# Linear attention and a maxout layer on one core: transposes from TensorE to crossbar DMAs, stores over all DMA engines, state sums by 64-row tiles

## The chip, the cores and the metric

One core of a Trainium2 chip runs the whole program. The metric is the device time of one execution in microseconds (us). A core has TensorE (PE, matmuls; PEld is its weight load), VectorE (DVE), ScalarE (ACT), GpSimd (POOL), SyncE (SP, here the queue that issues most of the DMAs), and 16 DMA engines. Each engine runs its own instructions strictly in order and waits at semaphores for the others.

## The reference, cut to what matters

```
B, H, S, D = 4, 8, 768, 48
state = zeros(B, H, D, D)
for t in range(S):
    cur = einsum('bhd,bhe->bhde', u * k[t], v[t])
    y[t] = einsum('bhd,bhde->bhe', r[t], state + cur)
    state = w[t][..., None] * state + einsum('bhd,bhe->bhde', k[t], v[t])
x = y as (B*S, H*D) = (3072, 384)
out = maximum(x @ w1, x @ w2) @ w_out          # d_ff = 1024
```

The recurrence is computed by chunks of C = 256 time steps. Inside a chunk, r' = r * exp(sum of log w so far) and k' = k * exp(-that sum) turn the decay into plain products. The maxout is computed as relu(x (w1 - w2)) w_out + x (w2 w_out).

## The kernel before, in words

There are 12 units of work, n = 0 to 11: chunk c = n // 4 of batch row b = n % 4, all 8 heads, 256 time steps. Two neighbouring steps lie in one partition (the index i), and a unit has two 64-partition halves (the index b of the code, Q = 64). A name such as `kp.5` is the operation `kp` on unit 5. The order in which all operations are issued is written out by hand in the string ORDER; every engine takes its own instructions in that order and never out of it. PSUM and SBUF tiles come from pools with fixed numbers of buffers.

The steps of a unit, with the engine of each:

- `w k r v`: loads of 384 KB each, issued by SP, three buffers each. `lw` (ACT) log w, `lp` (POOL) pair sums, `cs` (PE) running sums, `AE`, `AO`, `iA` (ACT) exponentials, `m`, `z` (DVE) sums.
- `rp`, `kp` (DVE, L262 and L266): r' and k' in bf16, both into `rkn_b`, two buffers. `rk`, `rku`, `vb`, `vd` (POOL) and `dg` (DVE): the part of the present step.
- `tr`, `evr` and `tk`, `evk`: r' and k' transposed by TensorE through an identity matrix, eight 128x128 transposes each (L317), into the single PSUM tile `tr`, and copied out by DVE (L330, L339) as `rT` and `kT`.
- `kv` (PE, L352): k'v into the PSUM tile `y`: j = 0 is the sum over the first 64 partitions, j = 1 the sum over all 128. `S1` (DVE, L362) is the state in the middle of the chunk, `Tf` (L369) at its end. `row`, `WL` (SP) and `Wt` (ACT) move one row of decays onto partitions through DRAM, `dec`, `S0` (POOL) decay the state.
- `sc0`, `sc1` (PE, L393): scores from `kT` and `rT`; `M0`, `M1` (DVE, L397): the mask. `yb`, `yi`, `ya` (PE, L413, L425, L437): the attention output, which `x` (ACT, L446) copies to SBUF.
- `xt`, `xT`: the attention output transposed by TensorE (L453, six 128x128 transposes) and copied out of PSUM by ACT (L458).
- `g0` to `g3` (PE, L466) and `r0` to `r3` (ACT, L474): 24 gate matmuls and the relus. `oc`, `oa`, `ob` (PE, L485, L490), `os` (ACT, L495) and `out` (SP, L500): two output blocks of 128 rows a unit, each stored as 192 KB.

Before the units run evenly, the weights come in: `w1` (SP), `w2` and `wo` (POOL DMAs that cast to bf16), `wd` (DVE, w1 - w2), `wt` (SP crossbar DMA, w2 transposed, three of 128x1024), `wcm` and `wce` (w2 w_out). Units overlap: while the attention of unit n + 2 is built, the gates and outputs of unit n run.

Of the kernel before, what the change touches and what calls it, by code (L numbers as in the profile page):

```python
# [17 lines left out]
w.0 k.0 lw.0 lp.0 cs.0 r.0 u v.0 w2 rk.0 rku.0 vb.0 AE.0 z.0 m.0 AO.0 rp.0 tr.0 iA.0 kp.0 evr.0  # L18
kv.0 Tf.0 tk.0 evk.0 dg.0 sc1.0 M1.0 S1.0 row.0 sc0.0 M0.0 vd.0 yb.0 yi.0 w1 w.1 lw.1 k.1 r.1
v.1 lp.1 wd.1 wd.0 wo w.2 cs.1 AE.1 m.1 AO.1 rp.1 z.1 row.1 wd.2 rk.1 rku.1 ya.0 x.0 tr.1 vb.1  # L20
wt.1 iA.1 k.2 r.2 v.2 w.3 wt.0 wt.2 xt.0 xT.0 g0.0 g1.0 r0.0 g2.0 r2.0 WL.1 WL.0 k.3 r.3 v.3 w.4
dg.1 vd.1 evr.1 kp.1 tk.1 evk.1 kv.1 Tf.1 S1.1 sc1.1 M1.1 yb.1 yi.1 k.4 r.4 v.4 lw.2 lp.2 w.5
cs.2 m.2 AE.2 z.2 row.2 AO.2 rp.2 iA.2 kp.2 sc0.1 M0.1 rk.2 rku.2 k.5 r.5 tr.2 evr.2 r1.0 g3.0
r3.0 wcm.1 wce.1 WL.2 lw.3 lp.3 ya.1 x.1 tk.2 evk.2 vb.2 dg.2 vd.2 v.5 w.6 wcm.0 wce.0 Wt.0 cs.3
m.3 AE.3 z.3 row.3 wcm.2 wce.2 sc0.2 M0.2 AO.3 rp.3 iA.3 kp.3 Wt.1 dec.1 S0.1 xt.1 xT.1 kv.2
Tf.2 S1.2 oc0.0 oa0.0 ob0.0 oc1.0 os0.0 out0.0 oa1.0 ob1.0 os1.0 out1.0 rk.3 rku.3 k.6 r.6 tr.3
evr.3 WL.3 sc1.2 M1.2 lw.4 lp.4 g0.1 g1.1 tk.3 evk.3 vb.3 r0.1 g2.1 r2.1 dg.3 vd.3 v.6 w.7 r1.1
yb.2 yi.2 ya.2 x.2 cs.4 m.4 AE.4 z.4 row.4 sc0.3 M0.3 AO.4 rp.4 g3.1 r3.1 oc0.1 oa0.1 iA.4 kp.4
xt.2 xT.2 kv.3 Tf.3 S1.3 ob0.1 oc1.1 os0.1 oa1.1 ob1.1 g0.2 out0.1 dec.0 S0.0 rk.4 rku.4 k.7 r.7
tr.4 evr.4 WL.4 sc1.3 M1.3 lw.5 lp.5 os1.1 g1.2 out1.1 r0.2 g2.2 r1.2 tk.4 evk.4 vb.4 r2.2 dg.4  # L30
vd.4 v.7 w.8 yb.3 yi.3 ya.3 x.3 cs.5 m.5 AE.5 z.5 row.5 sc0.4 M0.4 AO.5 rp.5 g3.2 r3.2 oc0.2
oa0.2 iA.5 kp.5 xt.3 xT.3 kv.4 Tf.4 S1.4 ob0.2 oc1.2 os0.2 out0.2 oa1.2 ob1.2 g0.3 rk.5 rku.5
k.8 r.8 tr.5 evr.5 WL.5 sc1.4 M1.4 lw.6 lp.6 Wt.2 dec.2 S0.2 os1.2 g1.3 out1.2 r0.3 g2.3 r1.3
tk.5 evk.5 vb.5 r2.3 dg.5 vd.5 v.8 w.9 yb.4 yi.4 ya.4 x.4 cs.6 m.6 AE.6 z.6 row.6 sc0.5 M0.5
AO.6 rp.6 g3.3 r3.3 oc0.3 oa0.3 iA.6 kp.6 xt.4 xT.4 kv.5 Tf.5 S1.5 ob0.3 oc1.3 os0.3 out0.3
oa1.3 ob1.3 g0.4 rk.6 rku.6 k.9 r.9 tr.6 evr.6 WL.6 sc1.5 M1.5 lw.7 lp.7 Wt.3 dec.3 S0.3 os1.3
g1.4 out1.3 r0.4 g2.4 r1.4 tk.6 evk.6 vb.6 r2.4 dg.6 vd.6 v.9 w.10 yb.5 yi.5 ya.5 x.5 cs.7 m.7
AE.7 z.7 row.7 sc0.6 M0.6 AO.7 rp.7 g3.4 r3.4 oc0.4 oa0.4 iA.7 kp.7 xt.5 xT.5 kv.6 Tf.6 S1.6
ob0.4 oc1.4 os0.4 out0.4 oa1.4 ob1.4 g0.5 rk.7 rku.7 k.10 r.10 tr.7 evr.7 WL.7 sc1.6 M1.6 lw.8
lp.8 Wt.4 dec.4 S0.4 os1.4 g1.5 out1.4 r0.5 g2.5 r1.5 tk.7 evk.7 vb.7 r2.5 dg.7 vd.7 v.10 w.11  # L40
yb.6 yi.6 ya.6 x.6 cs.8 m.8 AE.8 z.8 sc0.7 M0.7 AO.8 rp.8 g3.5 r3.5 oc0.5 oa0.5 iA.8 kp.8 xt.6
# [12 lines left out]
oc1.9 os0.9 out0.9 oa1.9 ob1.9 g0.10 kv.11 S1.11 os1.9 g1.10 out1.9 r0.10 g2.10 r1.10 r2.10
yb.11 yi.11 ya.11 x.11 g3.10 r3.10 oc0.10 oa0.10 xt.11 xT.11 ob0.10 oc1.10 os0.10 out0.10 oa1.10
ob1.10 os1.10 out1.10 g0.11 g1.11 r0.11 g2.11 r1.11 r2.11 g3.11 r3.11 oc0.11 oa0.11 ob0.11
oc1.11 os0.11 out0.11 oa1.11 ob1.11 os1.11 out1.11
# [22 lines left out]
def _body(tc, r, k, v, w, u_in, moe_w1, moe_w2, moe_w_out, out):  # L80
# [179 lines left out]
    @op  # L260
    def rp(n):
        nc.vector.tensor_mul(rkn_b[n % 2][:, 0, :, :, 0:D], byi(U[n]["r"]), U[n]["A"])  # L262

    @op
    def kp(n):
        nc.vector.tensor_mul(rkn_b[n % 2][:, 1, :, :, 0:D], byi(U[n]["k"]), U[n]["iA"])  # L266
# [46 lines left out]
    def transp(n, x):  # L313
        tp = pt_([P, NP, 2, 2, Q], BF16, "tr")
        for i in range(2):
            for p in range(NP):
                nc.tensor.transpose(  # L317
                    tp[:, p, :, i, :],
                    rkn_b[n % 2][:, x, i, 2 * p:2 * p + 2, :].rearrange("s r d -> s (r d)"),
                    ident)  # L320
        return tp

    @op
    def tr(n):
        U[n]["tr"] = transp(n, 0)

    @op
    def evr(n):
# [1 line left out]
        nc.vector.tensor_copy(t, U[n]["tr"])  # L330
# [4 lines left out]

    @op
    def evk(n):
        U[n]["kT"] = t = wt_([P, NP, 2, 2, Q], BF16, "kT")
        nc.vector.tensor_copy(t, U[n]["tk"])  # L339
# [3 lines left out]
    def kv(n):  # L343

        U[n]["kv"] = kp = pt_([P, 2, 512], F32, "y")
        for j in range(1 if last(n) else 2):
            q = slice(0, Q if j == 0 else P)
            for i in range(2):
                for p in range(NP):
                    for e in range(2):  # L350
# [1 line left out]
                        nc.tensor.matmul(  # L352
# [194 lines left out]
```

## Time and profile before

| | |
|---|---|
| time, three runs | 189.21, 189.55, 190.67 us (median 189.55) |
| the profiled execution | 190.6 us, of which the span of the profile is 188.8 us |
| PE busy | 148.2 us, 78% of the span |
| DVE, POOL, ACT busy | 124.8 us, 106.4 us, 88.3 us |
| mean granted TensorE clock | 0.965 |

The profiled execution is 1.8 us longer than the span; that part lies outside what the trace shows. It is 1.05 us above the median of the three runs. Busy matmul time is modelled and overlaps weight loads; what ends a stretch is read from the chain of work that ended last.

### The profile page before, as it was taken

The page shows a single profiled execution, that of the slowest core. Times are in us where ns is not written, and L with a number is a line of the kernel's source. Part 1 is how long each engine was busy: PE and PEld are TensorE (multiplying, and loading weights), DVE is VectorE, ACT ScalarE, POOL GpSimd, SP SyncE. Part 2 cuts the span into 40 slices and gives each one's busy share as a digit, 9 for nine tenths or more (in the row PEclk, how much of TensorE's full clock was granted, in tenths as well). Part 3 has the DMA queues.
Part 4 walks back from the last instruction along what each step waited for, and adds up shares of the span by engine and source line. Part 5 has one row for each costly group of instructions (what it writes and reads, how often), then busy time and mean ns, then how long its engine had stood idle before and what let it go on. Part 6 is the DMA issues. An engine that isn't in the chain of part 4 may idle for free.

```text
span 188.8 us, 4945 instructions
## 1 busy us (share of the span) xinstructions
PE 148.2 (78%) x2080; PEld 102.7 (54%) x2080; DVE 124.8 (66%) x173; ACT 88.3 (47%) x153; POOL 106.4 (56%) x96
## 2 busy tenths in 40 slices
PE   0345347849999999999999999999958599999400
PEld 0133116616567676776767668676746376767200
DVE  7478759466787798988979799798774776200000
ACT  3120134333436766748575574857642355456200
POOL 3853594272489994969878686983039970300000
PEclk9999999996999999999999999999999999999955
DMA  6999998999995568164574476457411111111110
GB/s 161 240 235 366 238 170 137 320 125 309 320 257 152 169 145 234 35 179 121 124 191 126 115 191 162 107 158 198 122 48 50 54 50 54 50 54 47 50 50 32
DMA packets 62454, 28.07 MB, mean 149 GB/s; under 512 B 57432, under 2 KB 61656, under 8 KB 62432
## 3 DMA queue, kind: packets, MB, share of 16 engines
q1 hardware_dynamic: 60992, 26.19, 51.3%
q0 software_dynamic: 1440, 1.57, 5.7%
q8 instruction: 16, 0.26, 0.6%
q14 instruction: 6, 0.05, 0.1%
HBM read 23.81 MB, written 4.73 MB: 151 GB/s over the span
## 4 chain that ended last, share of the span: by engine, by line
PE 54%; issue 6%; POOL 5%; DMA 4%; DVE 2%; ACT 2%; SPq 1%; DVEq 0%; POOLq 0%; ACTq 0%
PE go L466 14%; PE go L490 14%; PE go L485 5%; PE tr L317 4%; DMA lw<-in_w_dram 4%; PE y L352 3%; PE ex L235 3%; PE sc L393 3%; PE y L437 2%; PE y L413 2%; PE go L214 2%; PE y L425 2%; PE ex L453 2%; POOL rku L293 1%; POOL rku L298 1%
## 5 line engine op out<-in xcount | busy, mean ns | idle before, releaser
L466 PE MATMUL go<-xT,wd_sb 128*128 128x256 bf16 x288 | 40.1, 285 | 0.9 <-ACT xT L458 0.9
L474 ACT ACTIVATE gT<-go 128x512 bf16<-128x512 f32 x48 | 28.5, 595 | 18.3 <-PE go L466 17.7
L490 PE MATMUL go<-wo_sb,gT 128*128 128x384 bf16 x192 | 36.8, 326 | 0.0
L466 PEld LDWEIGHTS <-wd_sb 128*128 128x128 bf16 x288 | 27.6, 102 | 7.9 <-issue 1.1
L397 DVE TENSOR_TENSOR M<-sc,mask 128x1024 bf16<-128x1024 f32 x24 | 29.3, 1220 | 3.2 <-PE sc L393 2.7
L309 POOL TENSOR_TENSOR vd<-lv,dg 128x768 bf16<-128x768 f32 x12 | 17.7, 1474 | 23.9 <-DVE dg L304 21.0
L230 POOL TENSOR_TENSOR lp<-lw 128x384 f32<-128x384 f32 x12 | 16.9, 1411 | 17.9 <-ACT lw L225 17.9
L298 POOL TENSOR_TENSOR rku<-rku,u_b 128x768 f32<-128x768 f32 x12 | 24.1, 2010 | 0.9
L317 PE MATMUL tr<-ident,rkn 128*128 128x128 bf16 x192 | 16.7, 237 | 9.8 <-DVE rkn L262 9.6
L490 PEld LDWEIGHTS <-gT 128*128 128x128 bf16 x192 | 18.0, 98 | 11.4
L293 POOL TENSOR_TENSOR rku<-lr,lk 128x768 f32<-128x768 f32 x12 | 22.5, 1876 | 0.2
L262 DVE TENSOR_TENSOR rkn<-lr,A 128x768 bf16<-128x768 f32 x12 | 20.0, 1664 | 2.1 <-ACT A L253 2.1
L317 PEld LDWEIGHTS <-rkn 128*128 128x128 bf16 x192 | 14.0, 107 | 12.3 <-DVE rkn L262 11.0
L495 ACT COPY osb<-go 128x384 f32<-128x384 f32 x24 | 11.5, 479 | 19.2 <-PE go L490 16.6
L266 DVE TENSOR_TENSOR rkn<-lk,iA 128x768 bf16<-128x768 f32 x12 | 19.3, 1604 | 1.3 <-ACT iA L258 1.3
L235 PE MATMUL ex<-lp,triS 128*128 128x384 f32 x24 | 12.2, 595 | 9.4 <-POOL lp L230 9.4
L288 POOL CAST vb<-lv 128x768 bf16<-128x768 f32 x12 | 11.3, 943 | 9.9 <-DMA lv<-in_v_dram 9.5
L225 ACT ACTIVATE lw<-lw 128x768 f32<-128x768 f32 x12 | 10.1, 844 | 13.2 <-DMA lw<-in_w_dram 13.2
L485 PE MATMUL go<-wc_sb,xT 128*128 128x384 bf16 x72 | 15.6, 326 | 0.0
L446 ACT CAST x<-y 128x768 bf16<-128x768 f32 x12 | 9.6, 796 | 11.6 <-PE y L437 11.4
L241 ACT ACTIVATE A<-ex 128x384 f32<-128x384 f32 x12 | 5.9, 490 | 18.1 <-DVE mz L245 11.6
L304 DVE TENSOR_REDUCE dg<-rku 128x16 f32<-128x768 f32 x12 | 11.3, 944 | 3.1 <-POOL rku L298 3.1
(51 smaller groups left out, 188.6 us busy)
## 6 DMA issues: line engine op xcount, KB each, us to landing
lw<-in_w_dram SPq DMA_DIRECT2D x12, 384.0 KB
lk<-in_k_dram SPq DMA_DIRECT2D x12, 384.0 KB
lr<-in_r_dram SPq DMA_DIRECT2D x12, 384.0 KB
...
w_sb<-in_moe_w_dram POOLq DMA_DIRECT2D x1, 768.0 KB, 10.0
wo_sb<-in_moe_w_out_dram POOLq DMA_DIRECT2D x1, 768.0 KB, 7.4
```

The costliest lines, as they stand in the source:

```text
L235: nc.tensor.matmul(t.rearrange("p h d -> p (h d)"), triS, U[n]["lp"].rearrange("p h d -> p (h d)"))
L262: nc.vector.tensor_mul(rkn_b[n % 2][:, 0, :, :, 0:D], byi(U[n]["r"]), U[n]["A"])
L266: nc.vector.tensor_mul(rkn_b[n % 2][:, 1, :, :, 0:D], byi(U[n]["k"]), U[n]["iA"])
L293: nc.gpsimd.tensor_mul(t, U[n]["r"], U[n]["k"])
L298: nc.gpsimd.tensor_mul(t, t, u_b.rearrange("p (h d) -> p h d", h=H).unsqueeze(1).to_broadcast([P, 2, H, D]))
L309: nc.gpsimd.tensor_mul(t.rearrange("p i h d -> p h i d"), U[n]["v"], U[n]["dg"].to_broadcast([P, H, 2, D]))
L317: nc.tensor.transpose(tp[:, p, :, i, :], rkn_b[n % 2][:, x, i, 2 * p:2 * p + 2, :].rearrange("s r d -> s (r d)"), ident)
L397: nc.vector.tensor_mul(t.rearrange("s e p t -> s (e p) t"), U[n]["sc", i].rearrange("s e p t -> s (e p) t"), mask[:, i].rearrange("s i q - ...
L466: nc.tensor.matmul(g[:, f, :], wd_sb[:, ko, fo * P:(fo + 1) * P], U[n]["xT"][:, ko].rearrange("p j t -> p (j t)"), start=(f == 0 and ko == ...
L474: nc.scalar.activation(U[n]["gT"][:, 2 * j:2 * j + 2].rearrange("p f j t -> p f (j t)"), U[n]["g", j], AF.Relu)
L485: nc.tensor.matmul(t, U[n]["xT"][:, ko, b, :], wc_sb[:, ko, :], start=(ko == 0), stop=False)
L490: nc.tensor.matmul(U[n]["o", b], U[n]["gT"][:, fo, b, :], wo_sb[:, fo, :], start=False, stop=(fo == FO - 1))
```

## The change

What it does:

- k' is no longer transposed by TensorE: `evk` is one crossbar DMA on SP's queue from the SBUF tile `k_b` (128x1024 bf16) to `kT`. The matmuls `tk` and the DVE copy are gone.
- The attention output is transposed by one crossbar DMA on SP's queue too: `xT` reads `x` (128x768 bf16). The matmuls `xt` and the ACT copy are gone; the tile's axes are in another order, and so are the slices that the gates and `oc` read.
- r' is still transposed by TensorE; its copy out of PSUM, `evr`, moves from DVE to ACT.
- Each 128-row output block is stored by two DMAs of 64 rows whose outermost axis is the 64 rows; it was one DMA with an outermost axis of 2.
- `kv` sums each 64-partition half by itself (b = 0, 1), the halves in turns. `Sa` (DVE) adds the first half to the state, `S1` is now two copies of `Sa` to bf16, and `Tf` adds the second half to `Sa`.
- `WL` and `Wt` get three buffers, r' and k' tiles of their own, and the whole ORDER is new.

```diff
-    rkn_b = [const.tile([P, 2, 2, H, DP], BF16, name=f"rkn{i}") for i in range(2)]
+    r_b = [const.tile([P, 2, H, DP], BF16, name=f"rn{i}") for i in range(2)]
+    k_b = [const.tile([P, 2, H, DP], BF16, name=f"kn{i}") for i in range(2)]
...
-    def transp(n, x):
-        tp = pt_([P, NP, 2, 2, Q], BF16, "tr")
+    @op
+    def tr(n):
+        U[n]["tr"] = tp = pt_([P, NP, 2, 2, Q], BF16, "tr")
         for i in range(2):
             for p in range(NP):
                 nc.tensor.transpose(
                     tp[:, p, :, i, :],
-                    rkn_b[n % 2][:, x, i, 2 * p:2 * p + 2, :].rearrange("s r d -> s (r d)"),
-                    ident)
-        return tp
...
+                    r_b[n % 2][:, i, 2 * p:2 * p + 2, :].rearrange("s r d -> s (r d)"), ident)
     @op
     def evr(n):
         U[n]["rT"] = t = wt_([P, NP, 2, 2, Q], BF16, "rT")
-        nc.vector.tensor_copy(t, U[n]["tr"])
+        nc.scalar.copy(t, U[n]["tr"])
-    @op
-    def tk(n):
-        U[n]["tk"] = transp(n, 1)
     @op
     def evk(n):
-        U[n]["kT"] = t = wt_([P, NP, 2, 2, Q], BF16, "kT")
-        nc.vector.tensor_copy(t, U[n]["tk"])
+        U[n]["kT"] = t = wt_([P, 2, NP, P], BF16, "kT")
+        nc.sync.dma_start_transpose(out=t.rearrange("d i p q -> d (i p) q"),
+                                    in_=k_b[n % 2].rearrange("s i h d -> s (i h d)"))
...
     @op
     def kv(n):
         U[n]["kv"] = kp = pt_([P, 2, 512], F32, "y")
-        for j in range(1 if last(n) else 2):
-            q = slice(0, Q if j == 0 else P)
-            for i in range(2):
-                for p in range(NP):
-                    for e in range(2):
+        for i in range(2):
+            for p in range(NP):
+                for e in range(2):
+                    for b in range(1 if last(n) else 2):
                         h = 2 * p + e
+                        q = slice(b * Q, (b + 1) * Q)
...
+    @op
+    def Sa(n):
+        U[n]["Sa"] = t = wt_([P, NP, D], F32, "Sa")
+        nc.vector.tensor_add(t.rearrange("p q d -> p (q d)"), U[n]["kv"][:, 0, 0:NP * D],
+                             S_f[unit(n)[1]].rearrange("p q d -> p (q d)"))
...
-            nc.vector.tensor_add(S_1[n % 2][q, :, e * D:(e + 1) * D],
-                                 U[n]["kv"][q, 0, 0:NP * D].rearrange("p (q d) -> p q d", d=D),
-                                 S_f[unit(n)[1]][q])
+            nc.vector.tensor_copy(S_1[n % 2][q, :, e * D:(e + 1) * D], U[n]["Sa"][q])
...
-    def xt(n):
-        U[n]["xt"] = tp = pt_([P, KO, 2, P], BF16, "ex")
-        for b in range(2):
-            for ko in range(KO):
-                nc.tensor.transpose(tp[:, ko, b, :], U[n]["x"][:, b, ko * P:(ko + 1) * P], ident)
-
-    @op
     def xT(n):
-        U[n]["xT"] = t = wt_([P, KO, 2, P], BF16, "xT", 3)
-        nc.scalar.copy(t, U[n]["xt"])
+        U[n]["xT"] = t = wt_([P, 2, KO, P], BF16, "xT", 3)
+        nc.sync.dma_start_transpose(out=t.rearrange("p b k t -> p (b k) t"),
+                                    in_=U[n]["x"].rearrange("p b n -> p (b n)"))
...
-        nc.sync.dma_start(out=out[tok:tok + P, :].rearrange("(q i) n -> i q n", i=2),
-                          in_=U[n]["s", b])
+        for i in range(2):
+            nc.sync.dma_start(out=out[tok + i:tok + P:2, :],
+                              in_=U[n]["s", b][i * Q:(i + 1) * Q, :])
```

Of ORDER one line of the even part shows the new pattern: `k.6 WL.5 Wt.5 evk.5 sc1.5 M1.5 xT.4 g0.4 g1.4 r0.4 r1.4 vd.5 yb.5 sc0.5 M0.5 iA.6 kp.6 g2.4 r2.4`. What it moves is seen in the instructions of single engines.

SP's queue, one unit in the even part. Before (a unit's k and r loads, the decay row read back, one store, the next v and w loads, the decay row written, the other store):

```order
L176 DMA lk<-in_k_dram 128x8x96
L176 DMA lr<-in_r_dram 128x8x96
L277 DMA WL<-row 128x4x1
L500 DMA out_dram<-osb 2x64x384
L176 DMA lv<-in_v_dram 128x8x96
L176 DMA lw<-in_w_dram 128x8x96
L272 DMA row<-mz_91 1x512
L500 DMA out_dram<-osb 2x64x384
```

SP's queue at the same place in the changed kernel:

```order
L177 DMA lk<-in_k_dram 128x8x96
L278 DMA WL<-row 128x4x1
L331 DMA_TRANSPOSE kT<-kn_94 128x8x128
L447 DMA_TRANSPOSE xT<-x 128x6x128
L177 DMA lr<-in_r_dram 128x8x96
L177 DMA lv<-in_v_dram 128x8x96
L177 DMA lw<-in_w_dram 128x8x96
L273 DMA row<-mz_91 1x512
L491 DMA out_dram<-osb 64x384 x4
```

Two transposes now stand between the k load and the r load, each with a wait on DVE or ACT in front of it, and there are twelve DMAs a unit instead of eight. The loads were issued three to four units ahead of their use; k, r and v are now one unit ahead or less.

DVE, one unit in the even part. Before (from r' and k' to the second mask):

```order
L262 TENSOR_TENSOR rkn_92<-lr,A 128x16x48
L266 TENSOR_TENSOR rkn_92<-lk,iA 128x16x48
L369 TENSOR_TENSOR Tf_103<-y,Sf_99 128x192
L362 TENSOR_TENSOR S_111<-y,Sf_99 64x4x48 x2
L330 COPY rT<-tr 128x1024
L397 TENSOR_TENSOR M_1569<-sc,mask 128x1024
L339 COPY kT<-tr 128x1024
L304 TENSOR_REDUCE dg<-rku 128x16
L245 TENSOR_TENSOR mz_91<-ex,lw 128x8x48
L249 TENSOR_TENSOR mz_91<-ex,lp 128x8x48
L397 TENSOR_TENSOR M_1694<-sc,mask 128x1024
```

DVE in the changed kernel, one unit from k' to the second mask:

```order
L267 TENSOR_TENSOR kn_94<-lk,iA 128x16x48
L263 TENSOR_TENSOR rn_92<-lr,A 128x16x48
L305 TENSOR_REDUCE dg<-rku 128x16
L353 TENSOR_TENSOR Sa<-y,Sf_104 128x192
L360 CAST S_114<-Sa 64x4x48 x2
L364 TENSOR_TENSOR Tf_108<-y,Sa 128x192
L246 TENSOR_TENSOR mz_91<-ex,lw 128x8x48
L250 TENSOR_TENSOR mz_91<-ex,lp 128x8x48
L393 TENSOR_TENSOR M_1678<-sc,mask 128x1024
L393 TENSOR_TENSOR M_1723<-sc,mask 128x1024
```

Both copies out of PSUM are gone from DVE, k' comes before r', the two masks stand next to each other, and the two S1 instructions read SBUF instead of PSUM.

SP's queue at the start of the program, behind the first unit's loads. Before:

```order
L272 DMA row<-mz_90 1x512
L190 DMA w1f<-in_moe_w_dram 128x3x1024
L176 DMA lw<-in_w_dram 128x8x96
L176 DMA lk<-in_k_dram 128x8x96
L176 DMA lr<-in_r_dram 128x8x96
L176 DMA lv<-in_v_dram 128x8x96
L176 DMA lw<-in_w_dram 128x8x96
L272 DMA row<-mz_91 1x512
L206 DMA_TRANSPOSE w2T_sb<-w_sb 128x8x128
```

SP's queue at the start of the changed kernel:

```order
L177 DMA lw<-in_w_dram 128x8x96
L177 DMA lk<-in_k_dram 128x8x96
L207 DMA_TRANSPOSE w2T_sb<-w_sb 128x8x128
L331 DMA_TRANSPOSE kT<-kn_94 128x8x128
L177 DMA lr<-in_r_dram 128x8x96
L177 DMA lv<-in_v_dram 128x8x96
L177 DMA lw<-in_w_dram 128x8x96
L191 DMA w1f<-in_moe_w_dram 128x3x1024
L447 DMA_TRANSPOSE xT<-x 128x6x128
```

The first transpose of w2, which needs the w2 load, now stands in front of unit 0's k' and of unit 1's r and v loads. POOL's DMAs moved too. POOL before, from the w2 load to the w_out load (`w_sb` is w2):

```order
L194 DMA w_sb<-in_moe_w_dram 128x3x1024
L293 TENSOR_TENSOR rku<-lr,lk 128x768
L298 TENSOR_TENSOR rku<-rku,u_b 128x2x8x48
L288 CAST vb<-lv 128x768
L309 TENSOR_TENSOR vd<-lv,dg 128x8x2x48
L230 TENSOR_TENSOR lp<-lw 128x384
L198 DMA wo_sb<-in_moe_w_out_dram 128x8x384
```

POOL in the changed kernel, the same stretch:

```order
L195 DMA w_sb<-in_moe_w_dram 128x3x1024
L289 CAST vb<-lv 128x768
L231 TENSOR_TENSOR lp<-lw 128x384
L310 TENSOR_TENSOR vd<-lv,dg 128x8x2x48
L294 TENSOR_TENSOR rku<-lr,lk 128x768
L299 TENSOR_TENSOR rku<-rku,u_b 128x2x8x48
L289 CAST vb<-lv 128x768
L310 TENSOR_TENSOR vd<-lv,dg 128x8x2x48
L231 TENSOR_TENSOR lp<-lw 128x384
L199 DMA wo_sb<-in_moe_w_out_dram 128x8x384
```

The w2 load now stands behind both `rku` products of unit 0, and the w_out load behind all of unit 1's POOL work and unit 2's `lp`. On PE, `wcm.0`, which reads w_out, stands in front of the first gate.

More of the change, by code (lines that the diff above doesn't have):

```diff
@@ L17 @@
 ORDER = """
[L18 to L41, printed above, removed]
@@ L54 @@
[L54 to L57, printed above, removed]
+w.0 k.0 lw.0 lp.0 cs.0 AE.0 m.0 r.0 u rk.0 rku.0 v.0 w.1 w2 k.1 vb.0 z.0 wt.0 AO.0 rp.0 tr.0
+iA.0 kp.0 kv.0 Sa.0 S1.0 lw.1 lp.1 cs.1 AE.1 m.1 AO.1 z.1 iA.1 dg.0 vd.0 kp.1 evk.0 evr.0 sc0.0
@@ new lines @@
+M0.0 Tf.0 sc1.0 M1.0 yb.0 yi.0 ya.0 x.0 r.1 rp.1 tr.1 rk.1 evr.1 rku.1 dg.1 v.1 w.2 lw.2 vb.1
+kv.1 Sa.1 vd.1 S1.1 Tf.1 yb.1 lp.2 cs.2 AE.2 w1 wo wd.2 wd.0 wd.1 wcm.0 wce.0 xT.0 g0.0 r0.0
+row.0 m.2 AO.2 z.2 evk.1 sc1.1 M1.1 g1.0 r1.0 wt.1 wcm.1 wce.1 WL.0 Wt.0 dec.0 S0.0 wt.2 wcm.2
+wce.2 k.2 sc0.1 M0.1 iA.2 kp.2 g2.0 r2.0 g3.0 r3.0 yi.1 ya.1 x.1 r.2 v.2 rk.2 vb.2 w.3 lw.3 rp.2
+rku.2 dg.2 oc0.0 oa0.0 ob0.0 oc1.0 os0.0 oa1.0 tr.2 evr.2 kv.2 Sa.2 S1.2 Tf.2 ob1.0 os1.0 row.2
+lp.3 cs.3 AE.3 k.3 WL.2 Wt.2 evk.2 sc1.2 M1.2 xT.1 g0.1 g1.1 r0.1 r1.1 row.1 m.3 AO.3 z.3 vd.2
@@ new lines @@
+os1.4 out1.3 k.7 WL.6 Wt.6 evk.6 sc1.6 M1.6 xT.5 g0.5 g1.5 r0.5 r1.5 vd.6 yb.6 sc0.6 M0.6 iA.7
+kp.7 g2.5 r2.5 g3.5 r3.5 dec.5 S0.5 r.7 v.7 rk.7 vb.7 w.8 lw.8 rp.7 rku.7 dg.7 yi.6 ya.6 x.6
+oc0.5 oa0.5 ob0.5 oc1.5 os0.5 tr.7 evr.7 kv.7 Sa.7 S1.7 Tf.7 row.7 lp.8 cs.8 AE.8 m.8 AO.8 z.8
+out0.4 oa1.5 ob1.5 os1.5 out1.4 k.8 WL.7 Wt.7 evk.7 sc1.7 M1.7 xT.6 g0.6 g1.6 r0.6 r1.6 vd.7
+yb.7 sc0.7 M0.7 iA.8 kp.8 g2.6 r2.6 g3.6 r3.6 dec.6 S0.6 r.8 v.8 rk.8 vb.8 w.9 lw.9 rp.8 rku.8
+dg.8 yi.7 ya.7 x.7 oc0.6 oa0.6 ob0.6 oc1.6 os0.6 tr.8 evr.8 kv.8 Sa.8 S1.8 lp.9 cs.9 AE.9 m.9
```

73 lines of the change are left out of this document (42 added, 31 removed).

## The prediction

> **What bounds the kernel now.** I read the strip of 40 slices first, then a whole unit of the even part as a window, then the chain of work that ended last, then the end of the program.
>
> ```profile
> PE   0345347849999999999999999999958599999400
> DMA  6999998999995568164574476457411111111110
> ```
>
> ```profile
> 75.71:87.10 11.39, 11.39 (x182) 8.15 (x184) 10.25 (x13) 7.19 (x14) 9.63 (x9) 1.00 0.39 97
> 178.00:180.00 2.00, 0.00 (x0) 0.00 (x0) 0.00 (x0) 0.00 (x0) 0.00 (x0) 0.74 0.13 49
> ```
>
> The windows' columns are length, busy time of PE, PEld, DVE, ACT and POOL, granted clock, DMA share, GB/s. In the even part a unit takes 11.39 us, PE is busy for all of it at full clock, and DVE (10.25) and POOL (9.63) are not far behind. So PE is the bound there, with about 10% of room before DVE would be. The first 40 us are another matter: PE is half idle and the DMA engines are full. In the last 12 us only a DMA share of 0.13 is left, which is two engines of 16, at 49 GB/s.
>
> The chain through one unit, from one `kv` to the next:
>
> ```profile
> 52.10 0.73 PE y L352 x32
> ...
> 75.71 0.73 PE y L352 x32
> ...
> 77.68 1.30 PE go L490 x8
> ...
> 79.64 0.45 PE tr L317 x8
> 80.08 0.35 PE sc L393 x16
> 80.43 1.42 PE go L466 x12
> 81.85 0.45 PE tr L317 x8
> 82.29 0.44 PE y L413 x4
> ...
> 83.17 0.51 PE y L437 x32
> 83.68 0.84 PE ex L235 x2
> ...
> 86.77 0.34 PE ex L453 x6
> ...
> 175.36 1.31 PE go L490 x8
> ...
> 177.04 0.48 ACT osb L495
> ```
>
> **PE's work per unit.** The change removes one of the two `tr` groups (0.45) and the `xt` group (0.34). `kv` keeps 32 small matmuls, 0.73 before; in the new form four of them stand on different quarters of the array where two did. The nearest row is `ya`, also 32 matmuls of 48 columns on 64 rows, at 0.51. I take 0.2 off, between 0 and 0.37 (half), for units 0 to 7 only, since the last chunk sums one half in both kernels. PE then needs 11.39 - 0.45 - 0.34 - 0.2 = 10.4 us a unit. From unit 2's `kv` on, ten `tk` (4.5), ten `xt` (3.4) and six shorter `kv` (1.2) go: **-9.1 us**.
>
> **The tail.** PE ends at 176.67 and the last store lands at 188.8, 12.1 us later.
>
> ```profile
> 133.71 44.35 SPq L500 DMA_DIRECT2D out_dram<-osb x12
> ```
>
> ```profile
> L500 SPq DMA_DIRECT2D out_dram<-osb x24: 511/532/3762, 56.1 to 177.5; - x24
> ```
>
> ```profile
> 0.74 0.46 SPq L176 DMA_DIRECT2D lw<-in_w_dram  x1
> ...
> 4.21 0.84 ACT L225 ACTIVATE lw<-lw 128x768 f32<-128x768 f32 x1 [2.20 <-DMA lw<-in_w_dram]
> ```
>
> Stores wait in line from 133 us on: 0.2 MB at 49 GB/s is 4 us each, so 24 of them fill two engines for 96 us. With 64 rows outermost I expect all 16 engines, as for the loads, and no backlog. Then the tail is 0.33 (issue) and 0.48 (copy), two issues of 0.53, and a landing. The first load, alone, was there 3.5 us after its issue began, for four times the bytes; I take 2.6. That is 4.5 us, with 3 and 12.1 as bounds: **-7.6 us**.
>
> **The late loads.** The same backlog starves the last loads.
>
> ```profile
> 140.02 0.82 POOL L288 CAST vb<-lv 128x768 bf16<-128x768 f32 x1 [9.49 <-DMA lv<-in_v_dram]
> ```
>
> ```profile
> 142.32 0.51 PE L413 MATMUL y<-vd,sel 64*128 64x384 bf16 x4 [2.71 <-POOL vd L309]
> ...
> 148.84 0.43 PE L352 MATMUL y<-vb,rkn 64*64 64x48 bf16 x16 [2.02 <-POOL vb L288]
> ```
>
> PE stood still for 2.71 + 2.02 because unit 10's v came 9.5 us late. Without the backlog this goes: **-4.7 us**.
>
> **The crossbar DMAs.** The trace has three of evk's shape, `wt`.
>
> ```profile
> L206 SPq DMA_TRANSPOSE w2T_sb<-w_sb x3: 1311/1347/2529, 29.3 to 37.1; - x3
> ```
>
> ```profile
> DMA packets 413, 0.11 MB, mean 211 GB/s; under 512 B 413, under 2 KB 413, under 8 KB 413
> ```
>
> ```profile
> DMA packets 860, 0.33 MB, mean 326 GB/s; under 512 B 860, under 2 KB 860, under 8 KB 860
> ```
>
> The first was issued at 29.31; the middle row is 31.0 to 31.5, while it moved (266 B a packet), the last a microsecond of loads (384 B). So 0.26 MB take some 1.3 to 1.8 us of all engines, not more than a load of 0.39 MB (1.2) by much, and SP is held 1.35 us, 2.53 at worst. From the start of the issue to landed I take 3.1 us. Both DMAs of a unit (1.3 and three quarters of it), four loads (1.2 each) and two stores (0.39 MB at 16 times the 25 GB/s that an engine of the tail moves) come to 2.3 + 4.8 + 1.0 = 8.1 us of DMA time, below 10.4, so the loads still fit.
>
> The Trainium skill ("VectorE: DVE Perf Modes", section "The three transpose paths") speaks against the change: it gives 390 ns for a 128x128 bf16 transpose on TensorE and 1309 ns on the crossbar, and prefers TensorE where PSUM will do. By that figure taken per block, the 14 blocks of a unit would be an estimated 18.3 us; the trace's eight blocks in under 2 us do not agree.
>
> Is the latency covered? `xT.n` must land before `g0.n`. On SP it stands behind `evk`, which waits for `kp`. From the mask: mask 1.22, `kp` 1.6, two issues 2.7, landing 1.8, then `g0 g1` 1.42, `yb` 0.44, `sc0` 0.35, hand-overs 0.25, and the next mask: a loop of 9.8 us, 0.6 below PE's 10.4. Covered, barely.
>
> **What gives back.** A second loop runs through the same masks: mask, `kp`, `rp`, `tr`, `kv`, `cs`, `oa ob`, `sc1`, `g0 g1`, `yb`, `sc0`, mask.
>
> ```profile
> L397 DVE TENSOR_TENSOR M<-sc,mask 128x1024 bf16<-128x1024 f32 x24 | 29.3, 1220 | 3.2 <-PE sc L393 2.7
> ...
> L262 DVE TENSOR_TENSOR rkn<-lr,A 128x768 bf16<-128x768 f32 x12 | 20.0, 1664 | 2.1 <-ACT A L253 2.1
> ...
> L266 DVE TENSOR_TENSOR rkn<-lk,iA 128x768 bf16<-128x768 f32 x12 | 19.3, 1604 | 1.3 <-ACT iA L258 1.3
> ```
>
> ```profile
> 121.54 1.81 POOL L298 TENSOR_TENSOR rku<-rku,u_b 128x768 f32<-128x768 f32 x1
> 123.74 1.29 POOL L230 TENSOR_TENSOR lp<-lw 128x384 f32<-128x384 f32 x1 [0.38 <-ACT lw L225]
> ```
>
> ```profile
> 121.57 2.60 DVE L262 TENSOR_TENSOR rkn<-lr,A 128x768 bf16<-128x768 f32 x1
> 124.09 1.75 DVE L266 TENSOR_TENSOR rkn<-lk,iA 128x768 bf16<-128x768 f32 x1
> ```
>
> Here `rp` begins with a POOL product, ends 0.82 after it, and `kp` does the same behind `lp`: the two engines take turns whole instructions long. Without the PE part the pair costs 1.9 (alone: 0.82 each and a start), 3.27 (mean of all units) or 4.3 us (both shut out, as here). The PE part is 0.45 + 0.51 + 0.84 + 1.30 + 0.35 + 1.42 + 0.44 + 0.35 = 5.66, the mask 1.22, hand-overs 0.25. The loop is 9.0, 10.4 or 11.4 us. In the new order the pair meets POOL's `rk`, `vb`, `rku`, which begin when the r load lands, so I choose between the mean and the worst: 10.85 us a unit, 0.45 above PE's own work, for nine units: **+4.0 us** (0 to +9).
>
> DVE itself sheds the two copies and gains `Sa`:
>
> ```profile
> L339 DVE COPY kT<-tr 128x1024 bf16<-128x1024 bf16 x12 | 8.3, 689 | 4.1 <-PE tr L317 4.1
> L330 DVE COPY rT<-tr 128x1024 bf16<-128x1024 bf16 x12 | 8.2, 687 | 2.6 <-PE tr L317 2.4
> L362 DVE TENSOR_TENSOR S<-y,Sf 64x192 bf16<-64x192 f32 x24 | 8.4, 351 | 2.1 <-PE y L352 1.8
> ```
>
> 10.25 - 1.38 + 0.35 is 9.2 us, if the S1 copies cost about what the sums did (0.35 each). ACT exchanges one copy for another. The S1 copies have no like in the trace beside POOL work: 0 to 1.8 us each (a POOL product's length), and I take 0.35; at 1.8 each DVE would need 12.1 us and be the bound. The Trainium skill ("SBUF — State Buffer", section "SBUF: two separate sides") says that a DVE copy within SBUF in a two-port mode excludes GpSimd for the whole instruction, and the other way round. No row of this trace shows it for copies; by that rule the upper end would be the nearer one.
>
> **The start.** Here SP waits for w2 before it gives out unit 0's `evk` and unit 1's r.
>
> ```profile
> w_sb<-in_moe_w_dram POOLq DMA_DIRECT2D x1, 768.0 KB, 10.0
> wo_sb<-in_moe_w_out_dram POOLq DMA_DIRECT2D x1, 768.0 KB, 7.4
> ```
>
> ```profile
> 8.92 1.80 POOL L298 TENSOR_TENSOR rku<-rku,u_b 128x768 f32<-128x768 f32 x1
> ```
>
> POOL now issues w2 after unit 0's `rku`, at about 10.3 (the row's end, less 0.4 since the DMA no longer precedes it). It lands 7.4 to 10 us later, at 17.7 to 20.3. Two transposes are issued (2.7), then r.1 (0.6, landing 3): 24 to 26.6. Then `rk.1`, `rku.1`, `dg.1`, `vd.1` and `lp.2`, about 1.9 + 2.0 + 0.9 + 1.5 + 1.4, before POOL issues w_out at 32 to 34.5; it lands 7.4 later. PE, in order, holds at `wcm.0` until 39.4 to 42, and from there to unit 2's `kv` come 11.7 us of matmuls (three `wcm` at the 1.30 of eight matmuls of that size, 24 gates, and the groups of the chain), some 2.3 of waits for copies and masks, and 1.3 for a clock that drops when PE stands still (0.74 in the last window above), both my estimates: 54.7 to 57.3, against 52.1 before. PE will have done 2.1 us more by then (outputs of unit 0: 2.9, less one `cs`). At 56 that is 3.9 - 2.1: **+1.9 us** (0 to +4). At the end `xT.11` may show for **+0.5**.
>
> **Sum**, against the profiled execution of 190.6: -9.1 - 7.6 - 4.7 + 4.0 + 1.9 + 0.5 = -15.0, so 175.6. That execution is 1.05 above the median, so beside the median of 189.55 it is **174.5 us**.
>
> **The rivals.**
>
> - *Nothing is given back* (22%). The pair meets POOL idle, and PE stays the bound at 10.4: 174.5 - 4 = 170.5. For it: POOL waits for the r load, so `rk` may start behind `kp`. Against it: the pair's mean of 3.27 was reached with POOL less busy per us than it would be here (9.6 us of work in 10.4 instead of 11.4).
> - *DVE and POOL become the bound* (20%). The pair shut out each time gives 11.4 a unit, 174.5 + 9 x 0.55 = 179.5; with the S1 copies shut out as well, 12.1, it is 186. For it: POOL's 9.6 and DVE's pair leave little room. Against it: the pair's mean is well below the worst. The rule of the Trainium skill on the shared side of SBUF belongs to this case.
> - *Slower* (6%). The transposes land late: both issues at the worst 2.53 and a landing of 3.5 behind loads make the first loop 1.22 + 2.6 + 5.06 + 3.5 + 2.2 + 0.25 = 14.8 us, and the kernel 174.5 + 9 x 4 = 210. It is slower than before from a loop of 12.5 on. Against it: SP has drained its stores by the time that `kp` releases `evk`.
> - *The crossbar works block by block* (2%). With 1.35 us, the issue time of one, for each of 14 blocks, 18.9 us a unit, some 250 us; the 2 us of the trace's eight blocks speak against it. The Trainium skill's 1309 ns a block would be this case.
> - The forecast keeps 50%.
>
> **Range and chances.** 167 to 184 holds the forecast's own bounds (unit 10.4 to 11.3, start 0 to +4, tail 3 to 6), the first rival and most of the second. Faster by over 1% (about what a measurement of this kernel can tell from no change): 0.90; within it 0.02; slower 0.08, the last two rivals.
>
> **What would show it.** Right: the last store within 5 us of PE's end at a DMA share well above 0.13; no PE wait on `vd` or `vb` in units 10 and 11; a unit at 10.4 to 11.3; PE idle before L215 until about 40 us. Wrong: `g0` waiting for `xT` or `sc1` for `kT` in most units (first loop), or an even part at 11.4 or more.

## The result and the profile after

The changed kernel takes **180.63 us** (median of four runs, 180.04 to 182.59), the kernel before 190.11 beside it (189.21 to 191.04): ratio 0.952, 95% interval 0.943 to 0.961. It is faster by some 9.5 us; the forecast was 174.5 with a range of 167 to 184. The profiled execution has a span of 178.3 us, 180.1 with the 1.8 outside of it; the prediction's sum for that execution was 175.6. Times below leave out slow executions, over 1.5% above the fastest of the same kernel (one of four with the old stores, two of four in three other runs).

The strip of 40 slices, from the changed kernel's page:

```profile
PE   0324064505999987978998889989999999999990
DMA  5988799699925979998889879999999988171513
```

The long run of 1s in the DMA row, the stores' backlog, is gone, and with it the 12 us behind PE's end. In the even part the DMA engines now read 8 or 9 where they read 4 to 7, and PE reads 7 or 8 in several slices where it read 9.

Three windows, each from unit 2's `kv` to the end of PE (columns as in the prediction: length, busy time of PE, PEld, DVE, ACT, POOL, clock, DMA share, GB/s). Before:

```profile
52.10:176.67 124.57, 119.60 (x1740) 84.26 (x1740) 89.06 (x107) 71.85 (x128) 79.08 (x68) 1.00 0.45 121
```

After:

```profile
56.16:173.74 117.58, 109.67 (x1609) 72.69 (x1608) 91.78 (x102) 75.05 (x128) 80.34 (x67) 1.00 0.83 190
```

The kernel before with the new stores alone (an experiment below):

```profile
51.22:171.03 119.81, 119.53 (x1742) 84.15 (x1740) 89.37 (x107) 71.81 (x128) 79.68 (x68) 1.00 0.52 133
```

These rows hold the answer. PE's work went from 119.60 to 109.67 us, nearly as planned. But PE's idle time, 5.0 us before (the late loads), is 7.9 us after (117.58 - 109.67), where the stores alone bring it down to 0.3. The DMA share nearly doubles. For most of the time that PE was spared, it now stands still.

Units of the changed kernel, from one `kv` to the next:

```profile
90.10:101.80 11.70, 10.50 (x169) 6.89 (x171) 10.36 (x12) 7.40 (x13) 9.24 (x11) 1.00 0.88 213
...
112.95:124.35 11.40, 10.50 (x167) 6.96 (x168) 10.06 (x12) 7.51 (x13) 9.40 (x9) 1.00 1.04 211
...
135.30:145.90 10.60, 10.48 (x153) 6.88 (x154) 9.27 (x11) 7.41 (x12) 8.31 (x6) 1.00 0.92 233
```

In the first two rows PE's work of a unit is 10.5 us, and it takes 11.4 to 11.7 to get done. In the third row it takes 10.6: in the last chunk nothing is left to decay, POOL has 8.3 us of work instead of 9.2 to 9.4, and DVE has 9.3 instead of 10.1 to 10.4. The nine units from 56.16 to 156.30 take 10.1 to 12.5 us, 11.13 on average.

The chain of the changed kernel in that part:

```profile
85.98 1.01 DVE kn L267
86.99 2.50 DVE rn L263
...
89.53 0.62 PE tr L319 x8
90.15 0.37 PE y L344 x32
...
100.85 1.30 SPq L447
...
102.20 4.06 DMA lr<-in_r_dram
...
106.43 1.82 POOL rku L294
...
109.01 2.49 POOL rku L299
...
136.11 1.05 DVE S L360
...
137.47 0.57 DVE mz L246
...
138.49 0.47 ACT osb L485
...
139.00 0.81 PE go L456 x6
```

Before, the chain from 52 us to the end of PE was made of PE rows but for the stretch from 118 to 149 us, where the late loads stood in it. Now it goes from engine to engine. Around 100 us it passes k' and r' on DVE, PE, SP issuing `xT`, the r load that stands behind it on SP, and POOL's products that waited for r. From unit 8 on it passes `Sa`, `S1` and `m` on DVE and the output's copy on ACT, which frees the buffer of the next gate.

What PE waited for in this stretch, three of thirteen rows:

```profile
79.18 0.91 PE L236 MATMUL ex<-lp,triS 128*128 128x384 f32 x2 [1.17 <-POOL lp L231]
...
101.21 0.62 PE L319 MATMUL tr<-ident,rn 128*128 128x128 bf16 x8 [0.47 <-DVE rn L263]
...
105.42 1.47 PE L456 MATMUL go<-xT,wd_sb 128*128 128x256 bf16 x12 [0.73 <-DMA xT<-x]
```

Added up, PE waited 1.9 us for `xT`, 1.8 for r', 1.7 for the output's copies, 1.2 for `lp` and 0.9 for `kT`, 7.5 of its 7.9 us. No single wait decides: several loops of nearly the same length hold each other.

### The profile page after: what moved, and what is told of

The parts are those of the page before. It is cut to its first block, busy times and chain, and to the rows that moved or that the text cites. A ratio compares the mean times of both kernels' runs of the same rounds, so it can differ in the third digit from the quotient of the medians.

```text
span 178.3 us, 4629 instructions
## 1 busy us (share of the span) xinstructions
PE 135.8 (76%) x1912; PEld 87.9 (49%) x1912; DVE 126.7 (71%) x163; ACT 91.7 (51%) x153; POOL 106.8 (60%) x96
## 4 chain that ended last, share of the span: by engine, by line
PE 33%; DMA 24%; DVE 17%; POOL 12%; issue 6%; SPq 4%; ACT 2%; POOLq 0%; ACTq 0%
PE go L456 11%; PE go L480 7%; DVE rn L263 6%; DMA wo_sb<-in_moe_w_out_dram 5%; POOL rku L299 5%; DVE S L360 4%; DMA w_sb<-in_moe_w_dram 4%; DMA xT<-x 4%; PE go L475 3%; DMA u_b<-in_u_dram 3%; DMA out_dram<-osb 3%; PE go L215 3%; DVE kn L267 3%; DMA lw<-in_w_dram 2%; DMA lr<-in_r_dram 2%
## 5 line engine op out<-in xcount | busy, mean ns | idle before, releaser
L456 PE MATMUL go<-xT,wd_sb 128*128 128x256 bf16 x288 | 37.4, 276 | 3.8 <-DMA xT<-x 1.9
L393 DVE TENSOR_TENSOR M<-sc,mask 128x1024 bf16<-128x1024 f32 x24 | 29.3, 1219 | 12.8 <-PE sc L389 12.7
L480 PE MATMUL go<-wo_sb,gT 128*128 128x384 bf16 x192 | 35.3, 326 | 0.0
L294 POOL TENSOR_TENSOR rku<-lr,lk 128x768 f32<-128x768 f32 x12 | 21.8, 1814 | 20.2 <-issue 10.5
L456 PEld LDWEIGHTS <-wd_sb 128*128 128x128 bf16 x288 | 26.9, 99 | 10.5 <-issue 4.9
L299 POOL TENSOR_TENSOR rku<-rku,u_b 128x768 f32<-128x768 f32 x12 | 28.2, 2350 | 0.4 <-DMA u_b<-in_u_dram 0.3
L480 PEld LDWEIGHTS <-gT 128*128 128x128 bf16 x192 | 18.6, 98 | 14.1 <-issue 1.8
L263 DVE TENSOR_TENSOR rn<-lr,A 128x768 bf16<-128x768 f32 x12 | 25.1, 2095 | 0.1
L310 POOL TENSOR_TENSOR vd<-lv,dg 128x768 bf16<-128x768 f32 x12 | 17.7, 1475 | 11.2 <-DVE dg L305 10.7
L267 DVE TENSOR_TENSOR kn<-lk,iA 128x768 bf16<-128x768 f32 x12 | 18.6, 1550 | 0.1
L236 PE MATMUL ex<-lp,triS 128*128 128x384 f32 x24 | 13.0, 631 | 7.4 <-POOL lp L231 7.4
L360 DVE CAST S<-Sa 64x192 bf16<-64x192 f32 x24 | 17.6, 734 | 0.6
L389 PE MATMUL sc<-rT,kT 48*64 48x128 bf16 x384 | 10.7, 232 | 8.3 <-DMA kT<-kn 7.0
L326 ACT COPY rT<-tr 128x1024 bf16<-128x1024 bf16 x12 | 12.1, 1010 | 9.0 <-PE tr L319 9.0
L389 PEld LDWEIGHTS <-kT 48*64 48x64 bf16 x384 | 6.7, 112 | 17.0 <-DMA kT<-kn 8.9
```

The costliest lines, as they stand in the source:

```text
L263: nc.vector.tensor_mul(r_b[n % 2][:, :, :, 0:D], byi(U[n]["r"]), U[n]["A"])
L267: nc.vector.tensor_mul(k_b[n % 2][:, :, :, 0:D], byi(U[n]["k"]), U[n]["iA"])
L294: nc.gpsimd.tensor_mul(t, U[n]["r"], U[n]["k"])
L299: nc.gpsimd.tensor_mul(t, t, u_b.rearrange("p (h d) -> p h d", h=H).unsqueeze(1).to_broadcast([P, 2, H, D]))
L310: nc.gpsimd.tensor_mul(t.rearrange("p i h d -> p h i d"), U[n]["v"], U[n]["dg"].to_broadcast([P, H, 2, D]))
L360: nc.vector.tensor_copy(S_1[n % 2][q, :, e * D:(e + 1) * D], U[n]["Sa"][q])
```

## The experiments

**The new stores alone, in the kernel before.**

```
-        nc.sync.dma_start(out=out[tok:tok + P, :].rearrange("(q i) n -> i q n", i=2), in_=U[n]["s", b])
+        for i in range(2):
+            nc.sync.dma_start(out=out[tok + i:tok + P:2, :], in_=U[n]["s", b][i * Q:(i + 1) * Q, :])
```

> The kernel before with one part of the change alone: each output block stored by two DMAs of 64 rows with the rows outermost. By the prediction's terms the tail (7.6 us) and the late loads (4.7 us) go and nothing else moves: 177 to 178.5 us, which would be the whole gain of the change and more. Rival (the transposes and the new order have a share of the gain, and the even part of before has hidden waits behind its full store queue that stay): 181 to 184 us.

Measured 177.39 us (176.35 to 178.28), ratio 0.938 (0.931 to 0.946). This small part of the change is worth 12 us, as much as its two terms of the sum (7.6 and 4.7), and more than the entire change: its slowest time lies below the changed kernel's fastest (180.04), though the intervals of the two ratios overlap. The rival expectation, 181 to 184, did not come. Its units take 11.39 us with PE busy throughout:

```profile
97.69:109.08 11.39, 11.39 (x182) 8.15 (x184) 9.95 (x13) 7.19 (x14) 8.81 (x9) 1.00 0.61 158
```

**The rest of the change without the new stores:** the reverse of that edit, in the changed kernel.

> The changed kernel with each output block stored by one DMA as before (outermost axis of 2). Theory (the stores are worth the tail and the late loads): 24 stores of 4 us on two engines take 96 us, and the first one is ready at about 59 us, so the tail comes back and the transposes wait behind stores on these two engines: 190 to 198 us. Rival (the stores matter little): 181 to 184 us.

Measured 225.59 us (224.89 to 226.81), ratio 1.195 (1.180 to 1.210): far beyond either expectation. The chain, and SP's own rows:

```profile
94.66 8.45 DMA WL<-row
```

```profile
94.66 3.84 SPq L278 DMA_DIRECT2D WL<-row  x1
98.60 3.57 SPq L331 DMA_TRANSPOSE kT<-kn  x1
```

The small transfer `WL` needs 8.45 us from its issue to landing (4.8 for one in the changed kernel), and SP is held 3.84 and 3.57 us by issues that took 0.5 to 1.5 and 1.25 to 2.5 in the changed kernel's even part. The backlog is back: behind PE's end the DMA share is 0.13 again, two engines of 16. The next unit's loads stand behind these issues; PE waits 33.3 us for `kT`, and POOL 49.8 for r. So the backlog, which cost 12 us while nothing in the loop passed through SP, costs 45 once something does.

**S1 summed from PSUM**, as before the change, in the changed kernel.

```
-            nc.vector.tensor_copy(S_1[n % 2][q, :, e * D:(e + 1) * D], U[n]["Sa"][q])
+            nc.vector.tensor_add(S_1[n % 2][q, :, e * D:(e + 1) * D],
+                                 U[n]["kv"][q, 0, 0:NP * D].rearrange("p (q d) -> p q d", d=D), S_f[unit(n)[1]][q])
```

> The changed kernel with the two S1 instructions as they were before (DVE sum of the kv tile in PSUM and the state, not a copy of Sa in SBUF). Theory (DVE and POOL shut each other out, and the S1 copies at a mean of 734 ns are in the loop that sets a unit's length): S1 falls to about 0.35 us each, and eight units of the even part lose up to 0.75 us each; 174.5 to 176.5 us against 180.6. Rival (the loop over SP, the r load and POOL sets it, the DMA engines being full): no change, 180 to 181 us, DVE only idles more.

The groups of the changed kernel, and then the same line in this run:

```profile
L263 DVE TENSOR_TENSOR rn<-lr,A 128x768 bf16<-128x768 f32 x12 | 25.1, 2095 | 0.1
...
L360 DVE CAST S<-Sa 64x192 bf16<-64x192 f32 x24 | 17.6, 734 | 0.6
```

```profile
L360 DVE TENSOR_TENSOR S<-y,Sf 64x192 bf16<-64x192 f32 x24 | 8.4, 350 | 0.2
```

The copies took 734 ns on average, against the 350 that I had taken, and the sums 350. Yet the time was 179.13 us (178.52 to 179.45), ratio 0.947 (0.941 to 0.954), only 1.5 less, where 4 to 6 had been expected: 9.2 us of DVE work went, and most of it did not set the pace. DVE now waits 15.3 us for the scores instead of 12.7, and `rn` takes 2240 ns.

**AO of units 4 to 11 behind `os1`** on ACT, so that the output's PSUM buffer is free sooner (`... z.4 AO.4 ... os1.1` becomes `... z.4 ... os1.1 AO.4`).

> The changed kernel with the exponential AO of units 4 to 11 issued on ACT behind the copy os1 instead of ahead of it. Theory that ACT holds the output buffer (AO waits for DVE's m, and os1, which frees the PSUM tile for the second gate, stands behind it): the 0.3 to 0.7 us that PE waits for os1 in units 4, 5, 8 and 9 go, 1 to 3 us in all, 178 to 179.5 us. Rival (the same DVE chain holds the masks and k', so the wait only moves to tr): 180 to 181 us.

Measured 179.44 us (179.08 to 180.03), ratio 0.950 (0.943 to 0.957), 1.2 less, at the edge of what was expected.

**Both of these edits.**

> The changed kernel with both edits that helped a little alone: S1 summed from PSUM (179.1) and AO behind os1 (179.4). If each loop adds its own wait the gains add: 180.6 - 1.5 - 1.2 = 177.9. If another loop of nearly the same length sets the unit in any case (loads behind the transposes on SP, then POOL's products): 178.8 to 179.5.

Measured 178.39 us (177.31 to 179.84), ratio 0.938 (0.932 to 0.944), 2.2 less. The gains nearly add, but the two expectations lie closer together than the runs scatter. By the intervals of the ratios, neither edit alone nor both together are told apart from the changed kernel. Even with both, PE is idle for 7.2 us between unit 2's `kv` and its end, and the chain still runs over the r and w loads, POOL's products and a `rn` of 2.50.

**The r and v loads ahead of the transposes** on SP, for units 4 to 11 (`k.4 ... r.4 v.4` becomes `k.4 r.4 v.4`).

> The changed kernel with the r and v loads of units 4 to 11 issued right behind the k load, ahead of the two transposes, instead of behind them. Theory that the loop over SP (transposes, r load) and POOL (rk, rku, then dg and vd) holds the unit: POOL's waits for the r load (some 15 us in all) go, 177 to 178.5 us. Rival (DVE's turn-taking with POOL and the S1 copies hold it, or the transposes now come later behind 0.8 MB of loads): 180 to 183 us.

Measured 181.86 and 184.52 us, 1 to 4 more; the ratio, 0.970 (0.956 to 0.984), is not told apart from the changed kernel's, but the expected gain of 2 to 4 is not there.

```profile
L263 DVE TENSOR_TENSOR rn<-lr,A 128x768 bf16<-128x768 f32 x12 | 15.4, 1286 | 0.1
```

```profile
PE sc L389 <- DMA kT<-kn: 13.2, 5, 6.5
```

POOL waits 2.6 us for r instead of 9.1, and its products no longer meet `kp` and `rp`: from unit 4 on these take 0.95 us each, the best case of the prediction's second loop. Yet PE stands still for 11.1 us from unit 2's `kv` on, more than in the changed kernel: 6.8 of them for `kT` and 1.5 for `xT` (0.9 and 1.9 there). So the turns of DVE and POOL are not all that holds a unit. With them gone the transposes, now issued behind two more loads, hold it.

**The transposes put into the old order**, each on top of the new stores. First the output's (`xT.n` right behind `x.n`, `xt` gone, units 2 to 11):

> The kernel before with the new stores and one more part: the attention output of units 2 to 11 transposed by the crossbar DMA, issued right behind x, in the old order with its loads three units ahead. Theory (a crossbar DMA saves PE its matmuls where nothing waits for it; here some 6 us of other matmuls lie between x and its first gate): ten times 0.34 us below the kernel with the new stores alone (177.4), 174 us. Rival (the DMA in the queue, waiting for x, delays loads that something waits for): 177 to 180 us.

Measured 214.70 and 215.07 us. Both expectations are missed by 35 us or more. SP's rows:

```profile
69.60 0.58 SPq L175 DMA_DIRECT2D lr<-in_r_dram  x1
80.14 0.37 SPq L276 DMA_DIRECT2D WL<-row  x1
...
83.56 1.80 SPq L460 DMA_TRANSPOSE xT<-x  x1
```

`x` was done at 75.0, its transpose was issued at 83.56 and landed 4.25 us later. SP had stood at `WL` for 10 us, for one of its two buffers (46.5 us of such waits for `Wt` in the whole run), with the transpose some places behind. PE waited 31.5 us for `xT`.

Then k' (with three buffers for `WL` and `Wt`):

> The kernel before with the new stores and k' of units 2 to 11 transposed by the crossbar DMA at the place of the old matmuls, old order otherwise (three buffers for WL and Wt). Theory: ten times 0.45 us of PE, 173 us; DVE loses a copy of 0.69 a unit as well. Rival (loads are delayed, or DVE and POOL hold the unit at 11.4 us): 176 to 180 us.

Measured 212.41 us, ratio 1.124 (1.114 to 1.133), where 173, or 176 to 180, had been expected. And the new stores, both transposes and the 64-row `kv` together in the old order (`S1` summed from PSUM and `evr` on DVE, as before the change):

> The kernel before, its old order, with all three parts: new stores, both transposes of units 2 to 11 by crossbar DMA, and kv by 64-row halves with S1 summed from PSUM as before. Theory (the parts are good, the new order and the S1 copies gave the gain back): 177.4 - 3.4 - 4.5 - 2.2 = 167 us, better than both kernels. Rival (with PE at 10.3 us a unit, DVE and POOL set the pace in any order): 172 to 176 us.

Measured 206.29 us, ratio 1.092 (1.082 to 1.102), where 167, or 172 to 176, had been expected. In both, PE waits for `kT`, 24.6 and 28.4 us. What SP itself waited for, in the run with all of them:

```profile
SPq L515 <- ACT osb L509: 41.7, 18, 4.8
```

Stores that wait for their rows stand in front of the transposes in SP's order. To test that, the same kernel with both stores of unit n behind `os1` of unit n + 1, in the order alone:

> The run with all parts in the old order (206.3 us), its only edit that both stores of unit n stand behind os1 of unit n+1, so that SP never waits for os with a transpose behind it. Theory, the transposes were late because stores that wait stood ahead of them in SP's order: the 28 us of PE's waits for kT go, the unit falls from about 13.5 to 10.5 to 11.5 us, 172 to 182. Rival, the transposes themselves are too long for the old order (issue 1.2 to 2.6 us and 3 to 4 us to land, between x and the gates, and between k' and the scores): 195 or more.

```profile
SPq L515 <- ACT osb L509: 2.9, 3, 1.6
```

The wait is nearly gone, and the times are 190.45 and 192.77 us, 14 to 16 less. The mechanism is right for about half of the loss against the new stores alone; the other half stayed, so the expected 172 to 182 was missed. SP's rows of this run, and the chain:

```profile
90.67 0.37 SPq L278 DMA_DIRECT2D WL<-row  x1
91.09 3.06 SPq L515 DMA_DIRECT2D out_dram<-osb  x4
94.20 1.33 SPq L343 DMA_TRANSPOSE kT<-kn  x1
```

```profile
94.20 3.12 DMA kT<-kn
```

k' was done at 87.9. SP then issued two loads (87.93 to 88.94), came to `WL` at 90.67, and needed 3.06 us for four stores that waited for nothing. The transpose began 6.3 us late, and its landing of 3.1 us stood bare in PE's chain.

The last run in the old order issues the stores from ScalarE instead, right behind the copies, and lags none:

> The same run (206.3 us), its only edit that the stores are issued by ScalarE, where they stand right behind the copy that makes their rows, and none by SP. Theory (stores that wait on SP hold the transposes): 172 to 182, as with lagged stores, plus what 48 issues cost ScalarE. Rival (the transposes' own length in the old order): 195 or more. If lagged stores help and this does not, issues on ScalarE are the cost.

Measured 196.55 us, ratio 1.032 (1.028 to 1.036), 9.7 less than with the stores on SP. That is the rival's 195 or more, not the expected 172 to 182. ACT pays: the issues appear in the chain, between the output's copies and the relus that PE waits for.

```profile
99.84 0.47 ACTq L515
```

No version with DMA transposes in the old order came below 190 us, where the changed kernel, with the same two transposes in the order that it writes out (both transposes first, then the loads, `row`, stores that lag a unit), takes 180.6. No run puts the old TensorE transposes into the new order, so the price of that order alone is not known.

**New stores and the 64-row `kv`, no transposes.**

```
-        for j in range(1 if last(n) else 2):
-            q = slice(0, Q if j == 0 else P)
...
+                    for b in range(1 if last(n) else 2):
+                        q = slice(b * Q, (b + 1) * Q)
...
+    def Sa(n):   # state + first half; Tf adds the second half to it; S1 stays a sum from PSUM
```

> The kernel before with the new stores and the 64-row halves of kv (and the state sums Sa, S1 from PSUM, Tf that go with them), nothing else: no transpose moves to a DMA, the order stays. In the changed kernel a kv takes 0.37 us where it took 0.73. If the kernel with the new stores alone (177.4 us) is bound by TensorE in its even part, some ten units give 0.36 each: 173.5 to 174.5, the fastest version so far. Rival: the added sum Sa and the waits of VectorE take it back, 176.5 to 178.

Measured 177.23 us (176.79 to 178.06), ratio 0.932 (0.928 to 0.936). It is not told apart from the new stores alone (0.938); its interval lies below that of the changed kernel. The expected gain of 3.6 did not come: from unit 2's `kv` on PE has 118.0 us of work instead of 119.5, and the stretch takes 120.0 instead of 119.8. A window in its even part, and the chain through one unit there:

```profile
97.69:109.08 11.39, 11.15 (x180) 7.82 (x178) 10.38 (x14) 7.15 (x14) 9.27 (x9) 1.00 0.61 156
```

```profile
97.48 1.22 DVE M L403
98.70 1.07 DVE rkn L263
99.77 2.49 DVE rkn L267
...
103.19 0.36 DVE S L368
103.58 0.70 DVE rT L331
104.32 0.61 PE tr L318 x8
...
106.31 0.86 PE ex L236 x2
107.27 0.57 DVE mz L246
107.86 0.50 ACT A L242
108.91 1.22 DVE M L403
```

PE has 0.24 us less to do in this window and the unit is as long as before, 11.43 from one mask to the next. The chain is now a loop through DVE, with a `kp` of 2.49 that POOL's `rku` (99.03 to 101.44) shuts out, as the pair did in the prediction. The new `Sa` (102.26 to 102.54) adds 0.3 to this loop. Without it the loop would be an estimated 11.1 us at these durations, and by that estimate it stood in the kernel before too, just behind a PE of 11.39 that was busy to 100%.

## Why the prediction was right or wrong

The direction and the range held; the forecast was 4.5 us short against the profiled execution. The time lies at the lower end of the second rival's (*DVE and POOL become the bound*, 179.5 to 186, 20%), but its mechanism is shown only in part: `S1` shut out by POOL is worth some 1.5 us, and PE's waits are spread over five causes. Step by step:

- **Tail, -7.6: right.** PE ends at 173.74, `osb` is copied, and the last store lands 4.6 us after PE (forecast 4.5).

```profile
172.42 1.31 PE go L480 x8
...
173.80 0.48 ACT osb L485
```

- **Late loads, -4.7: right.** No wait of PE for `vd` or `vb` is left in units 10 and 11. The run with the stores alone confirms both terms by itself (12.3 expected, 12 to 13 measured): PE ends at 171.03 of 175.4, a tail of 4.4, and its idle time falls from 5.0 to 0.3.
- **The start, +1.9: right, with some luck.** Unit 2's `kv` came at 56.16 (56), from two errors that cancel: w_out took 9.7 us to land where 7.4 had been taken, and so landed at 42.1, the end of the forecast's 39.4 to 42; the stretch from there to `kv` took 14.1 us instead of 15.3.

```profile
32.36 9.74 DMA wo_sb<-in_moe_w_out_dram
```

- **PE's work, -9.1: about right.** From unit 2's `kv` on PE's busy time fell by 9.9; with the 2.1 that it does earlier, 11.2 had been forecast, 1.3 too much. `kv` became shorter than I took it to be (0.37, where 0.73 - 0.2 stood in the sum), which makes the gap 1.0 larger. On the other side, groups that start after a stop became longer: the transposes of r' that stay take 0.62 us in the chain, where such a group took 0.45 before, some 1.7 in ten units. The rest of the gap, an estimated 0.6, is not traced.
- **The transposes' latency, covered: not quite.** `g0` waited for `xT` 1.9 us in all, in four units, and `sc` for `kT` 7.0, of which 6.1 once, at the start. That leaves 2.8 us from unit 2's `kv` on, over a third of PE's idle time, where the sum had 0.5 for `xT.11`. Neither of the two low rivals happened. The price of standing behind waiting stores, which I argued away with SP having drained its stores, is real, as the old order showed; in the new order SP waits 7.2 us for the output's rows, against 41.7 in the old order with all three parts.
- **What gives back, +4.0: the step that failed, by its size.** PE's idle time is 7.9 us, where 4.0 + 0.5 stood in the sum. The unit is 11.13 us, not 10.85. The pair `rp`, `kp` took 2095 + 1550 ns on average over all units, 3.65, where the loop had 3.72 between mean and worst: that was well chosen. But the loop went from `kv` to the next mask over PE alone (`cs`, `oa`, `ob`, `sc1`). In the trace it also goes over DVE's `Sa`, `S1` and `m` and ACT's copy of the output, which the sum left out. `S1` was priced in DVE's own work only, at 0.35 each, and a copy took 0.73 on average. The rows of DVE and of POOL in unit 10:

```profile
146.70 1.39 DVE L360 CAST S<-Sa 64x192 bf16<-64x192 f32 x2
```

```profile
146.23 1.48 POOL L310 TENSOR_TENSOR vd<-lv,dg 128x768 bf16<-128x768 f32 x1 [0.15 <-DVE dg L305]
```

  The first copy does not end before POOL's `vd` is over (147.71), and both have ended 0.38 later. That is what the rule of the Trainium skill ("SBUF — State Buffer", section "SBUF: two separate sides") says of a copy within SBUF, and this trace agrees; I had noted that by it the upper end would be nearer, and still took the lower one. Summing S1 from PSUM instead gave only 1.5 us, so the rest of the miss isn't theirs: the loop that I summed was one of several with nearly the same length.
- **"The loads still fit", 8.1 us of DMA time in 10.4: wrong.** The DMA share from 66 to 135 us is 0.88 to 1.08, 0.97 on average, some 11 us a unit. Most of the miss is not the transposes': the loads and stores stood in the sum with 5.8 us, and the run with the stores alone shows 0.68 on average from 62 to 120 us, some 7.8 a unit. SP's queue is nearly as full: in the unit from 99.5 to 110.4 its issues add up to 10.1 us. Then r lands when POOL already waits for it, and moving it ahead makes `kT` late instead.

**Where the gain of the transposes went.** Against the run with the stores alone, the changed kernel starts its even part 4.9 us later (56.16 and 51.22), saves 9.9 us of PE's work, and gives 7.6 back as idle time: 178.3 against 175.4 for the span. The run with the new stores and the 64-row `kv` shows what it ran into: with 0.24 us less PE work in a unit, the unit did not become shorter. What stays open is which of the loops is the longest in the changed kernel. S1, AO and the place of the loads, each taken alone, move the time by 1 to 4 us; with the r and v loads early, POOL's part of the loop was gone, and the transposes held PE instead.
